# Moving two splits in the first batch of a fused attention and expert kernel

## The chip, the cores and the metric

The kernel runs on one core of one Trainium2 chip. The metric is the device time of one execution in microseconds (us), lower is better. The core has five engines that run side by side, each through its own queue in order: TensorE (PE, matrix products), VectorE (DVE), ScalarE (ACT), GpSimd (POOL) and SyncE (SP, which only issues transfers).

## The reference, cut to what matters

Three blocks follow one another. Four batches of 576 tokens go through an attention with 32 memory slots and 8 heads; its result, 512 numbers per token, goes through a dense MLP with a hidden width of 2048, and that result through 8 experts, two for each token.

```python
def _moe_ref(x, w_in, w_out):          # 2304 tokens, 512 -> 2048 -> 512
    h = x @ w_in
    g = h * (1.0 / (1.0 + np.exp(-h)))
    return (g @ w_out).astype(np.float32)
```

The change lies in this dense MLP, and in its first batch and the second.

## The kernel before, in words

Every float32 product is made from two parts: a number is split into a high part (a copy that is rounded to the format fp32r, by ACT) and a low part (the number less its high part, by DVE or POOL), and PE adds up three products, high by high, high by low and low by high.

The MLP of one batch is 32 steps, two for each of the 16 slices `f` of 128 hidden columns. Step `2f` takes the first 256 tokens of the batch (i = 0), step `2f + 1` the other 320 (i = 1). `mlp_h(b, f, i)` does one step: six matmuls into a PSUM tile `h` (L288), tanh by ACT (L291), the product `(tanh + 1) * h` by DVE (L293), then the split of 256 columns into `gh` (ACT, L297) and `gl` (DVE, or POOL in every fourth step of the first batch, L298). Where i = 1 the last 64 tokens are split as well, into half of a tile `gc` (ACT L306, DVE L307): the last 64 tokens of batches 0 and 1 share one tile of 128, so do those of batches 2 and 3. `mlp_x(b, f, i)` multiplies `g` with slice `f` of w_out (L313) and runs LAG = 4 steps behind `mlp_h`. The `gc` tiles are read by `mlp_rest` after the last step of batch 1 and of batch 3.

w_in and w_out arrive as float64 and are narrowed on the chip during the MLP of the first batch. One slice of w_out goes through `narrow_wout(f)` in step `2f - 1`: three ACT operations on the staged bits (L211, L212, L227), a join by DVE (L217), a multiplication with the sign by POOL (L232), and then the split into `woh[f]` (ACT, L275) and `wol[f]` (POOL for odd `f`, DVE for even, L276). The tile `wo` between them has two buffers. w_in comes in 8 chunks, `narrow_win` (ACT, DVE), and `project` multiplies it with the attention memory (PE L157, then ACT L263 and DVE L264, tile `wpl`).

In the same steps the attention of the next batch is prepared (`phi_top`, `phi_max`, `memory`, `scores`, `softmax_a`, `softmax_b`, `split`). Which function belongs to which step is written out by hand: `at(step, function, ...)` files it under a step, and each step runs `mlp_x`, `mlp_h` and then the functions filed under it. A scheduler afterwards sets the order of each engine's queue from this sequence and from its own estimate of when operands are ready; `tc.issue_after(x)` puts the instructions of a block behind `x` in the queue of x's engine.

Of the kernel before, what the change touches and what calls it, by code (L numbers as in the profile page):

```python
# [6 lines left out]
F32 = mybir.dt.float32  # L7
# [4 lines left out]
AF = mybir.ActivationFunctionType  # L12
OP = mybir.AluOpType
# [3 lines left out]
DM, FF, E, FE = 512, 2048, 8, 1024  # L17
# [3 lines left out]
NF = FF // 128  # L21
# [23 lines left out]
def body(ctx, tc, a):  # L45
    nc = tc.nc
    pe, act, dve, pool, sp = nc.tensor, nc.scalar, nc.vector, nc.gpsimd, nc.sync
# [8 lines left out]
    def psum(tag, bufs):  # L56
        return ps.tile([128, 512], F32, name=tag, tag=tag, bufs=bufs)
# [18 lines left out]
    m1 = moe1.enter_context(tc.tile_pool(name="m1", bufs=1))  # L76
    ap_ = att.enter_context(tc.tile_pool(name="att", bufs=1, side="right"))
# [108 lines left out]
    def turn(b, g, t0, w):  # L186
        AU[b, g] = ap_.tile([128, S], F32, name="att", bufs=2)
        return dve.transpose(AU[b, g][:, :w], AT[b][:, g].rearrange("p a m -> p (a m)")[:, t0:t0 + w])

    def halves(b, g, t0, w):  # L190
        u = AU.pop((b, g))[:, :w]
        if (b, g) not in AH:
            AH[b, g] = [m1.tile([128, S], F32R, name=f"ah{i}", bufs=3) for i in range(2)]
        hi, lo = (x[:, t0:t0 + w] for x in AH[b, g])
        last = act.activation(hi, u, AF.Copy)  # L195
        dve.tensor_sub(lo, u, hi.bitcast(F32))
        return last

    def split(b, g, t0, w):
        turn(b, g, t0, w)  # L200
        halves(b, g, t0, w)


    def stage(src):
        t = m1.tile([128, 512, 2], I32, name="st", tag="st", bufs=4)
        sp.dma_start(t.rearrange("p a w -> p (a w)").rearrange("p (c x) -> p c x", c=src.shape[1]), src)
        return t

    def shrink(t, m):
        low = ap_.tile([128, 512], I32, name="lw", bufs=1)  # L210
        act.activation(low, t[:, :, 0].bitcast(U32), AF.Copy, scale=LOW, bias=LOWB)  # L211
        act.activation(m, t[:, :, 1].bitcast(F32), AF.Copy, scale=2.0 ** -112)  # L212
        return low

    def join(m, low):
        mi = m.bitcast(I32)
        return dve.scalar_tensor_tensor(mi, mi, 3, low, op0=OP.logical_shift_left, op1=OP.bitwise_or)  # L217

    def sign(t, m):
        mi = m.bitcast(I32)  # L220
        dve.scalar_tensor_tensor(mi, t[:, :, 1], -2 ** 31, mi, op0=OP.bitwise_and, op1=OP.bitwise_or)

    def narrow(t, m, own=False):
        low = shrink(t, m)
        if not own:
            g = ap_.tile([128, 512], BF16, name="cg", bufs=1)
            act.activation(g, t[:, :, 1].bitcast(F32), AF.Sign)  # L227
        join(m, low)
        if own:
            sign(t, m)  # L230
        else:
            pool.tensor_mul(m, m, g)  # L232
# [36 lines left out]
    def fetch_wout(i):  # L269
        ST["o", i] = stage(wout[:, i:i + 1, :])  # L270

    def narrow_wout(i):
        w = ap_.tile([128, DM], F32, name="wo", bufs=2)
        narrow(ST.pop(("o", i)), w)
        act.activation(woh[i], w, AF.Copy)  # L275
        (pool if i % 2 else dve).tensor_sub(wol[i], w, woh[i].bitcast(F32))  # L276

    G, X2, GC = {}, {}, {}

    def mlp_h(b, f, i):  # L280
        t0, w = T0[i], TW[i]
        hi, lo = WP[(b * NP + f // 2) // 2]
        c = (f % 4) * 128
        p = psum("h", 2)
        n = 0
        for g in range(2):
            for wt, at in ((hi, 0), (hi, 1), (lo, 0)):
                pe.matmul(p[:, :w], wt[:, g, c:c + 128], AH[b, g][at][:, t0:t0 + w], start=(n == 0), stop=(n == 5))  # L288
                n += 1
        th = m1.tile([128, 320], F32, name="th", bufs=2)  # L290
        act.activation(th[:, :w], p[:, :w], AF.Tanh, scale=0.5)  # L291
        u = th
        dve.scalar_tensor_tensor(u[:, :w], th[:, :w], 1.0, p[:, :w], op0=OP.add, op1=OP.mult)  # L293
        if i == 0:
            G[b, f] = [m1.tile([128, MAIN], F32R, name=f"g{x}", bufs=LAG // 2 + 1) for x in "hl"]
        gh, gl = (x[:, i * 256:(i + 1) * 256] for x in G[b, f])
        act.activation(gh, u[:, :256], AF.Copy)  # L297
        last = (pool if b == 0 and (2 * f + i) % 4 == 0 else dve).tensor_sub(gl, u[:, :256], gh.bitcast(F32))  # L298
        if b:
            LATEST[0] = last  # L300
        if i == 1:
            if (b // 2, f) not in GC:
                GC[b // 2, f] = [m1.tile([128, 128], F32R, name=f"gc{f}_{x}") for x in range(2)]
            ch, cl = GC[b // 2, f]
            r = slice((b % 2) * 64, (b % 2) * 64 + 64)
            act.activation(ch[:, r], u[:, 256:], AF.Copy)  # L306
            dve.tensor_sub(cl[:, r], u[:, 256:], ch[:, r].bitcast(F32))  # L307

    def accumulate(key, terms, f):
        if f == 0:  # L310
# [568 lines left out]
        softmax_b(0, T0[1], TW[1])  # L879
    with tc.issue_after(ready.ins):  # L880
        narrow_wout(0)
    split(0, 0, T0[1], TW[1])
    split(0, 1, T0[1], TW[1])
    with tc.issue_after(ready.ins):
# [4 lines left out]
    def at(s, fn, *args):  # L889
        hooks.setdefault(s, []).append((fn, args))  # L890
# [6 lines left out]
    for f in range(1, NF):  # L897
        at(max(0, 2 * f - 5), fetch_wout, f)
        at(2 * f - 1, narrow_wout, f)
    SB = 2 * NF  # L900
    at(8, routing_setup)
    for b in range(1, B):
        s = (b - 1) * SB
        at(s + (1 if b > 1 else 4), load_phi, b)
# [25 lines left out]
        for i in range(0, NP, 2):  # L930
            for x in range(2):
                at(s + SB - 8 + 4 * i, fetch_win, b * NP + i + x)
            at(s + SB - 4 + 4 * i, project, b * NP + i, 2)
    for b in range(B - 1):
        s = (b + 1) * SB + LAG
        for d in range(4):
# [5 lines left out]
        if b == 1:  # L942
# [3 lines left out]
            at(s + 6, tile_d, j)  # L946
    s = 3 * SB
    at(s, open_a)
    at(s - SB + 10, clear)
    for j in range(EARLY):  # L950
# [8 lines left out]
    def run_h(s):  # L959
        if s < total:  # L960
            mlp_h(s // SB, s % SB // 2, s % 2)
# [19 lines left out]
    while s < total + LAG + 6:  # L981
# [4 lines left out]
        if s in (2 * SB, 4 * SB):  # L986
            b = s // SB - 1
# [83 lines left out]
```

## Time and profile before

| | us |
|---|---|
| median of three runs | 849.98 |
| lowest and highest of them | 848.54, 850.69 |
| the profiled execution, its own time | 845.91 |
| its span, first to last instruction | 844.1 |
| PE busy in the span | 807.1 |

The profile is of one execution. The span is shorter than the execution's own time by what lies around the first and the last instruction. "Busy" is the time in which an engine has an instruction running; instructions of one engine overlap a little at their ends. An "idle before" with an arrow names what the engine waited for.

### The profile page before, as it was taken

How to read it: one execution, taken by the hardware profiler on the slowest of the kernel's cores; microseconds unless marked ns; L12 is line 12 of the kernel's file. 1: busy time of each engine (PE TensorE's matmuls, PEld its weight loads, DVE VectorE, ACT ScalarE, POOL GpSimd, SP SyncE). 2: the span in 40 equal slices, each digit the busy share in tenths (PEclk: the TensorE clock that was granted, in tenths of full speed). 3: DMA queues.
4: the chain of work that ended last, by engine and by line, in shares of the span. 5: the costliest groups of instructions: out<-in, count | busy, mean ns of one | idle time of the engine just before them, and what ended most of it. 6: DMA issues, size and time to landing. Idle time of an engine off the chain costs nothing.

```text
span 844.1 us, 14185 instructions
## 1 busy us (share of the span) xinstructions
PE 807.1 (96%) x5260; PEld 691.4 (82%) x5260; DVE 496.8 (59%) x1178; ACT 360.8 (43%) x856; POOL 209.9 (25%) x237
## 2 busy tenths in 40 slices
PE   4589999999999999999999999999999999999996
PEld 2267678878887888887988989989989899898995
DVE  4898996884268747655724555354553654546521
ACT  3689975444333454553414433324332333233410
POOL 1254530021000400400541504215133142241301
PEclk9599999999999999999999999999999999999999
DMA  9889852543074215232456893765748647586201
GB/s 304 291 295 325 283 217 71 159 131 94 7 229 153 51 51 151 57 82 50 113 138 187 257 257 124 185 237 171 188 169 221 241 139 160 198 220 196 74 4 53
DMA packets 85935, 137.84 MB, mean 163 GB/s; under 512 B 14045, under 2 KB 48349, under 8 KB 85856
## 3 DMA queue, kind: packets, MB, share of 16 engines
q1 hardware_dynamic: 74656, 104.41, 40.9%
q0 software_dynamic: 11200, 32.43, 12.7%
q8 instruction: 43, 0.70, 0.4%
q14 instruction: 36, 0.29, 0.1%
HBM read 106.13 MB, written 31.26 MB: 163 GB/s over the span
## 4 chain that ended last, share of the span: by engine, by line
PE 81%; DVE 9%; ACT 4%; DMA 3%; issue 2%; POOL 1%; SPq 0%; POOLq 0%; ACTq 0%; DVEq 0%
PE x L706 25%; PE x L313 18%; PE x L682 13%; PE h L682 12%; PE h L288 9%; PE aux L157 2%; DMA st<-moe_w_out 1%; DVE th L293 1%; DVE gl L298 1%; DMA kx<-kx 1%; ACT lw L211 1%; POOL wo L232 1%; DMA st<-moe_w_in 1%; DVE mx L113 1%; DVE wo L217 1%
## 5 line engine op out<-in xcount | busy, mean ns | idle before, releaser
L706 PE MATMUL x<-w,gh 128*128 128x512 f32 (+1 forms) x608 | 188.1, 390 | 0.0
L706 PEld LDWEIGHTS x<-w,gh 128*128 128x128 f32 (+1 forms) x608 | 112.4, 186 | 24.3
L682 PE MATMUL h<-xh,w 128*128 128x304 f32 (+4 forms) x512 | 118.7, 304 | 0.0
L706 PE MATMUL x<-w,gl 128*128 128x512 f32 (+1 forms) x304 | 118.5, 390 | 0.0
L682 PE MATMUL x<-xh,w 128*128 128x304 f32 (+4 forms) x512 | 118.1, 302 | 0.0
L288 PE MATMUL h<-ah,wph 128*128 128x320 f32 (+1 forms) x512 | 109.3, 302 | 3.8 <-DVE th L293 1.7
L313 PE MATMUL x<-gh,woh 128*128 128x512 f32 x256 | 105.5, 412 | 0.0
L288 PEld LDWEIGHTS h<-ah,wph 128*128 128x128 f32 x512 | 90.0, 192 | 18.2 <-ACT ah L195 3.6
L721 POOL DMA_INDIRECT out<-y,tab x40 | 41.9, 1049 | 243.1 <-DVE y L716 187.3
L313 PE MATMUL x<-gl,woh 128*128 128x512 f32 x256 | 100.7, 393 | 0.7 <-DVE gl L298 0.7
L313 PE MATMUL x<-gh,wol 128*128 128x512 f32 x256 | 101.2, 395 | 0.0
L293 DVE SCALAR_TENSOR_TENSOR th<-th,h 128x256 f32<-128x256 f32 (+1 forms) x128 | 57.6, 450 | 53.0 <-ACT th L291 52.5
L497 POOL DMA_INDIRECT tab_d<-rows,slot x36 | 40.6, 1128 | 191.3 <-DVE slot L494 177.9
L682 PEld LDWEIGHTS h<-xh,w 128*128 128x128 f32 x512 | 87.3, 188 | 0.6
L682 PEld LDWEIGHTS x<-xh,w 128*128 128x128 f32 x512 | 87.4, 188 | 0.0
L291 ACT ACTIVATE th<-h 128x256 f32<-128x256 f32 (+1 forms) x128 | 52.3, 408 | 73.4 <-PE h L288 71.3
L288 PE MATMUL h<-ah,wpl 128*128 128x256 f32 (+1 forms) x256 | 76.6, 300 | 2.3 <-DVE wpl L264 2.3
L682 PE MATMUL x<-xl,w 128*128 128x304 f32 (+4 forms) x256 | 78.0, 305 | 0.0
L682 PE MATMUL h<-xl,w 128*128 128x304 f32 (+4 forms) x256 | 77.7, 303 | 0.0
L297 ACT ACTIVATE gh<-th 128x256 fp32r<-128x256 f32 x128 | 53.3, 416 | 55.7 <-DVE th L293 55.3
L298 DVE TENSOR_TENSOR gl<-th,gh 128x256 fp32r<-128x256 f32 x120 | 55.1, 459 | 32.0 <-ACT gh L297 28.1
L716 DVE SCALAR_TENSOR_TENSOR y<-x,tab,ex 128x512 f32<-128x512 f32 (+2 forms) x35 | 26.2, 749 | 71.4 <-PE x L706 71.4
(189 smaller groups left out, 1342.0 us busy)
## 6 DMA issues: line engine op xcount, KB each, us to landing
w2s<-moe_w SPq DMA_DIRECT2D x32, 512.0 KB, 8.5
wi<-win_d SPq DMA_DIRECT2D x24, 512.0 KB, 5.1
w1s<-moe_w SPq DMA_DIRECT2D x24, 512.0 KB, 6.2
kv<-kv SPq DMA_DIRECT2D x16, 520.0 KB, 7.3
st<-moe_w_in SPq DMA_DIRECT2D x16, 512.0 KB, 5.2
st<-moe_w_out SPq DMA_DIRECT2D x16, 512.0 KB, 5.9
xs_d<-ex SPq DMA_DIRECT2D x25, 256.0 KB, 3.6
x_d<-xs SPq DMA_DIRECT2D x36, 128.0 KB, 2.4
```

Of the source, the lines that this page charges most:

```text
L157: pe.matmul(p[g][h * M:(h + 1) * M], KVT[b][r, t, h * M:(h + 1) * M], moving(h)[r], start=True, stop=True)
L288: pe.matmul(p[:, :w], wt[:, g, c:c + 128], AH[b, g][at][:, t0:t0 + w], start=(n == 0), stop=(n == 5))
L291: act.activation(th[:, :w], p[:, :w], AF.Tanh, scale=0.5)
L293: dve.scalar_tensor_tensor(u[:, :w], th[:, :w], 1.0, p[:, :w], op0=OP.add, op1=OP.mult)
L297: act.activation(gh, u[:, :256], AF.Copy)
L298: last = (pool if b == 0 and (2 * f + i) % 4 == 0 else dve).tensor_sub(gl, u[:, :256], gh.bitcast(F32))
L313: pe.matmul(X2[key], held, moved, start=(f == 0 and n == 0), stop=(f == NF - 1 and n == 2))
L497: st = pool.indirect_dma_start(out=tab_d, out_offset=bass.IndirectOffsetOnAxis(ap=slot[:, j, k:k + 1], axis=0), in_=rows.bitcast(I32)[:, j ...
L682: pe.matmul(p[:, :w], wt[:, d, c], x[:, d, r], start=(n == 0), stop=(n == 11))
L706: mm = pe.matmul(p, g, w[:, f, :], start=(n == 0), stop=(n == (15 if both else 23)))
L716: done = dve.scalar_tensor_tensor(y, p[:P], w, EX[k, j], op0=OP.mult, op1=OP.add)
L721: st = pool.indirect_dma_start(out=a["out"], out_offset=bass.IndirectOffsetOnAxis(ap=TAB[k][:P, j, 0:1], axis=0), in_=y, in_offset=None, b ...
```

## The change

Two things are moved.

First, in batch 0 the last 64 tokens of each slice `f` are left unsplit in a wide tile `UR`, at a column offset that falls by 64 with each `f`, so that the next slice overwrites only the 256 columns that are done with. The split of slices 0 to 14 (`halve_rest`, one ACT and one DVE instruction each) is filed under steps 38 to 52, the steps 6 to 20 of batch 1, and queued behind the `gh` and `gl` of the step. Slice 15 is split at once, as are all slices of the later batches. The tile `th` with two buffers becomes `TH` for i = 0 and `UR` for i = 1.

Second, `narrow_wout` ends with POOL's multiplication; the split into `woh` and `wol` becomes `halve_wout(f)` and is filed one step later, under step `2f`.

```diff
     def narrow_wout(i):
-        w = ap_.tile([128, DM], F32, name="wo", bufs=2)
+        w = WO[i] = ap_.tile([128, DM], F32, name="wo", bufs=2)
         narrow(ST.pop(("o", i)), w)
+
+    def halve_wout(i):
+        w = WO.pop(i)
         act.activation(woh[i], w, AF.Copy)
         (pool if i % 2 else dve).tensor_sub(wol[i], w, woh[i].bitcast(F32))
 
+    TH = m1.tile([128, 256], F32, name="th")
+    UR = m1.tile([128, 256 + NF * 64], F32, name="ur")
+
+    def rest0(b, f):
+        return 256 if b else 256 + (NF - 1 - f) * 64
...
-        th = m1.tile([128, 320], F32, name="th", bufs=2)
-        act.activation(th[:, :w], p[:, :w], AF.Tanh, scale=0.5)
+        th = (UR[:, rest0(b, f) - 256:] if i else TH)[:, :w]
+        act.activation(th, p[:, :w], AF.Tanh, scale=0.5)
         u = th
...
-        act.activation(gh, u[:, :256], AF.Copy)
+        LAST[0] = act.activation(gh, u[:, :256], AF.Copy)
         last = (pool if b == 0 and (2 * f + i) % 4 == 0 else dve).tensor_sub(gl, u[:, :256], gh.bitcast(F32))
+        LAST[1] = last
...
-            ch, cl = GC[b // 2, f]
-            r = slice((b % 2) * 64, (b % 2) * 64 + 64)
-            act.activation(ch[:, r], u[:, 256:], AF.Copy)
-            dve.tensor_sub(cl[:, r], u[:, 256:], ch[:, r].bitcast(F32))
+            if b or f == NF - 1:
+                halve_rest(b, f)
+
+    def halve_rest(b, f, after=None):
+        u = UR[:, rest0(b, f):rest0(b, f) + 64]
+        ch, cl = GC[b // 2, f]
+        r = slice((b % 2) * 64, (b % 2) * 64 + 64)
+        with tc.issue_after(after[0].ins) if after else ExitStack():
+            act.activation(ch[:, r], u, AF.Copy)
+        with tc.issue_after(after[1].ins) if after else ExitStack():
+            dve.tensor_sub(cl[:, r], u, ch[:, r].bitcast(F32))
...
         narrow_wout(0)
+        halve_wout(0)
...
         at(2 * f - 1, narrow_wout, f)
+        at(2 * f, halve_wout, f)
     SB = 2 * NF
+    for f in range(NF - 1):
+        at(SB + 6 + f, halve_rest, 0, f, LAST)
```

## Rows read from the trace of the kernel before

**Rows 1.** The page: span, and each engine's busy time, share and instructions.

```profile
span 844.1 us, 14185 instructions
...
PE 807.1 (96%) x5260; PEld 691.4 (82%) x5260; DVE 496.8 (59%) x1178; ACT 360.8 (43%) x856; POOL 209.9 (25%) x237
```

**Rows 2.** Windows: length, busy PE, PEld, DVE, ACT, POOL (instructions), clock, DMA share, GB/s.

```profile
37.00:131.00 94.00, 86.25 (x624) 66.57 (x625) 86.08 (x167) 79.29 (x187) 40.83 (x38) 0.98 0.79 271
...
75.00:90.00 15.00, 14.87 (x101) 11.51 (x102) 11.94 (x27) 13.49 (x33) 6.72 (x8) 1.00 0.98 333
...
144.00:180.00 36.00, 35.23 (x313) 28.95 (x312) 28.92 (x103) 14.81 (x41) 2.07 (x2) 1.00 0.51 159
```

**Rows 3.** Waits of PE, 37 to 131: total us, times, longest.

```profile
PE h L288 <- DVE wpl L264: 2.3, 2, 1.2
PE h L288 <- DVE th L293: 1.7, 3, 0.8
...
PE x L313 <- DVE gl L298: 0.7, 1, 0.7
...
PE aux L122 <- DVE mt L120: 0.7, 1, 0.7
```

**Rows 4.** Waits of ACT, 37 to 131, same columns.

```profile
ACT woh L275 <- POOL wo L232: 5.4, 8, 1.2
...
ACT th L291 <- DVE gc L307: 0.4, 1, 0.4
```

**Rows 5.** Windows of L307 alone (DVE), then of L306 alone (ACT).

```profile
37.00:131.00 94.00, 8.31 (x16) 0.98 0.79 271
131.00:213.00 82.00, 3.48 (x16) 1.00 0.40 117
...
37.00:131.00 94.00, 3.97 (x16) 0.98 0.79 271
```

**Rows 6.** Timeline of DVE: start, length, instruction, wait before it.

```profile
43.20 1.19 DVE L307 TENSOR_TENSOR gc<-th,gc 128x64 fp32r<-128x64 f32 x1
...
46.04 1.64 DVE L217 SCALAR_TENSOR_TENSOR wo<-wo,lw 128x512 int32<-128x512 int32 x1
...
49.20 0.21 DVE L307 TENSOR_TENSOR gc<-th,gc 128x64 fp32r<-128x64 f32 x1
49.33 0.41 DVE L293 SCALAR_TENSOR_TENSOR th<-th,h 128x256 f32<-128x256 f32 x1
...
59.35 1.19 DVE L307 TENSOR_TENSOR gc<-th,gc 128x64 fp32r<-128x64 f32 x1
60.46 0.41 DVE L293 SCALAR_TENSOR_TENSOR th<-th,h 128x256 f32<-128x256 f32 x1
60.79 0.28 DVE L120 TENSOR_REDUCE mt<-aux 128x1 f32<-128x128 f32 x1
...
101.44 1.19 DVE L307 TENSOR_TENSOR gc<-th,gc 128x64 fp32r<-128x64 f32 x1
102.55 0.68 DVE L217 SCALAR_TENSOR_TENSOR wo<-wo,lw 128x512 int32<-128x512 int32 x1
...
124.61 1.19 DVE L307 TENSOR_TENSOR gc<-th,gc 128x64 fp32r<-128x64 f32 x1
```

**Rows 7.** Timeline of POOL.

```profile
45.83 1.31 POOL L276 TENSOR_TENSOR wol<-wo,woh 128x512 fp32r<-128x512 f32 x1 [1.51 <-ACT woh L275]
...
57.51 1.63 POOL L276 TENSOR_TENSOR wol<-wo,woh 128x512 fp32r<-128x512 f32 x1 [0.98 <-ACT woh L275]
59.10 1.36 POOL L232 TENSOR_TENSOR wo<-wo,cg 128x512 f32<-128x512 f32 x1
...
101.37 1.18 POOL L232 TENSOR_TENSOR wo<-wo,cg 128x512 f32<-128x512 f32 x1 [0.68 <-DVE wo L217]
```

**Rows 8.** Timeline of PE: first use of `wol` of slices 1 and 3.

```profile
48.21 0.40 PE L313 MATMUL x<-gh,wol 128*128 128x512 f32 x1
...
59.83 0.40 PE L313 MATMUL x<-gh,wol 128*128 128x512 f32 x1
```

## What the change was expected to do

> **What bounds the kernel now.** I read the page first. PE is busy for 807.1 of 844.1 us [rows 1], so over the whole kernel it is the bound, and a change on another engine can pay only where PE stands still. I then cut the span into windows to find those places. The MLP of the first batch, from 37 to 131 us, is the one that this change touches: 94 us with 86.25 busy on PE, so 7.75 us of standing still [rows 2]. In the same window DVE is busy for 86.08 us and ACT for 79.29 us, with the transfers at 0.79 of the DMA engines [rows 2]: no single engine is the bound there, PE and DVE are neck and neck, and ACT is close behind. From 75 to 90 us it is PE itself, 14.87 of 15 us [rows 2].
>
> Next I asked whom PE waits for in this window. Nearly all the waits name DVE: 2.3 us for `wpl`, 1.7 for the tanh product, 0.7 for `gl`, 0.7 for `mt` [rows 3]. With two more rows of the same view (0.7 and 0.3 us) PE's waits for DVE come to 6.4 us, six rows in all. So at the margin the work of DVE sets the end of this batch. Behind it PE goes on almost without a gap: 35.23 of 36 us from 144 to 180 us [rows 2]. What the first batch gains should therefore reach the end of the kernel.
>
> Then the waits of ACT: 5.4 us in eight waits of `woh` for POOL's multiplication [rows 4]. ACT's queue is in order, so the next tanh and the next `gh` stand behind each of these waits, and DVE waits for them in turn.
>
> Last, the timeline of DVE. The subtraction that makes the low part of `gc` writes 64 columns and takes 0.21 us when alone, and the next instruction starts 0.13 us after it [rows 6]. But five of the 16 in this window, the first at 43.20 and the last at 124.61, take 1.19 us [rows 6]. The one at 59.35 ends with POOL's multiplication that began at 59.10 and lasted 1.36 us, and the one at 101.44 with POOL's at 101.37, 1.18 us [rows 6, 7]. A subtraction with both inputs in SBUF waits there until POOL is done. That explains why 16 small subtractions cost 8.31 us here and 3.48 us in the second batch [rows 5]: 5 x 1.19 + 11 x 0.21 = 8.3.
>
> **The change, part by part.**
>
> *The 15 subtractions on DVE.* Those of slices 0 to 14 leave the window; that of slice 15, a short one, stays. Ten short ones at 0.13 us of the queue give 1.3 us. Five long ones hold the queue for 1.11 us each (59.35 to 60.46 [rows 6]), 5.55 us. Not all of it comes free: behind the one at 101.44 comes a join (L217) at 102.55 [rows 6], and a join also waits for POOL, for one of them took 1.64 us at 46.04 beside POOL's subtraction of 45.83 [rows 6, 7]. It would take over about 1.0 us of that wait. The one at 59.35 is followed by the tanh product, 0.41 us, which reads PSUM and shows no such wait [rows 6]; the other three are followed by the same instruction in the timeline, so I count them as free. The sum is 1.3 + 5.55 - 1.0 = 5.9 us of DVE. If all long waits are handed on, it is 15 x 0.13 = 2.0 us; if none, 6.9 us.
>
> *Why this reaches PE.* At 59.35 the long subtraction stands ahead of `mt` at 60.79, for which PE waits 0.7 us [rows 3, 6]. It also delays the next tanh product, from which PE's h matmuls get their PSUM tile. These gaps are bounded by the 6.4 us in which PE waits for DVE. From 75 to 90 us time on DVE buys nothing, since PE has no gap there: 79/94 of 5.9 us is 5.0 us.
>
> *The 15 copies on ACT.* They are 3.97 / 16 = 0.25 us each [rows 5], at most 3.7 us, and one of the DVE subtractions held up a tanh for 0.4 us [rows 4]. PE's own waits for ACT are small, so I count these at nothing by themselves: they pay by feeding DVE, whose 5.0 us is already counted. If that cover is wrong, and ACT is what holds DVE back, up to 6.4 us can be had in all.
>
> *`woh` and `wol` one step later.* Nothing is removed; the eight waits of ACT, 5.4 us, can be filled with the next step's tanh and `gh`. That too feeds DVE and is counted at nothing above the 5.0 us. Behind it is a danger: what is late next is `wol`. For slice 1 POOL ends it at 45.83 + 1.31 = 47.14 and PE reads it at 48.21, 1.07 us later; for slice 3 it is 57.51 + 1.63 = 59.14 and 59.83, 0.69 us [rows 7, 8]. The mean step is 94 / 32 = 2.9 us. The later slices are split further ahead of their use. If the scheduler keeps `woh` as soon as POOL's product is there, nothing is lost; a whole step later costs 1.8 + 2.2 = 4.0 us. No row shows which. The instruction only yields to work that is ready, so I am near the low end and take 0.5 us. The two buffers of `wo` are held a step longer, but the product that needs one back comes two slices later.
>
> *The 15 splits in batch 1.* They add 15 x 0.22 = 3.3 us to DVE (3.48 / 16 each [rows 5]) and 3.7 us to ACT between about 144 and 180 us. There DVE is busy 28.92 and ACT 14.81 of 36 us, and POOL, which made the waits, only 2.07 [rows 2]. PE's gap there is 0.77 us. What hides them is the four steps by which `mlp_x` runs behind. Uncovered they cost 15 x 0.13 = 2.0 us of DVE's queue; covered nothing. I take 0.5 us.
>
> *The tiles.* `TH` and `UR` are reused after two steps, as the two buffers of `th` were. No transfer is added or moved past another. I count nothing.
>
> The sum is 5.0 - 0.5 - 0.5 = 4.0 us. The profiled execution, 845.91 us with 1.8 us around its span, would become 841.9. It is 4.07 us faster than the median of the runs, 849.98, to which the forecast refers: **846.0 us**.
>
> **The rule that speaks against it.** The row shows 1.19 us beside POOL against 0.21 us alone [rows 6]. The Trainium skill says in "SBUF — State Buffer", section "Who interferes with whom", that a DVE instruction with two SBUF inputs contends with a GpSimd instruction that reads SBUF, and that the one issued second is blocked for the whole of the other. The trace agrees: 1.19 us ends with POOL's instruction. By that rule POOL's own instructions, which the change leaves as many and as long, block whichever such DVE instruction comes next, so the sum would be 2.0 us and not 5.9.
>
> **The rivals.**
>
> *The waits are handed on.* The place of each long subtraction is taken by the next `gl`, join or `wol` that meets POOL. For it: POOL works 40.83 of 94 us [rows 2], and the joins wait as well (1.64 us). Against: four of five times what follows reads PSUM. DVE gains 2.0 us, less 0.5 in batch 1: 848.5 us. It is what the rule above would make of it. Chance 0.20.
>
> *The staged transfers set the pace.* Then faster narrowing only waits for the next slice. For it: the DMA engines are at 0.98 from 75 to 90 us. Against: they are at 0.79 over the batch [rows 2], and no wait of PE leads straight to them. I give it a gain of 1 us, 849.0 us. Chance 0.10.
>
> *Slower: `wol` comes late.* With a lag of L for slices 1 and 3, PE loses 2L - 1.76 us. At one step this only eats the gain (849.98 - 4.5 + 4.0 = 849.5). It turns to slower by over 0.3% when 2L - 1.76 exceeds 4.5 + 2.55, so at L = 4.4 us, and at the 5.9 us of a whole slice it is 10.0 us, 855.5 us. For it: only about 1 us of room, and the split is filed behind the projection in its step. Against: POOL stood idle for 1.51 and 0.98 us before these two subtractions, waiting for ACT [rows 7], so for a lag of 4.4 us ACT would have to put other ready work ahead of `woh` for a step and a half. Chance 0.12.
>
> **How the numbers follow.** The forecast has 0.58. About 0.3%, 2.55 us, is what a measurement can tell here. Faster is the forecast alone, 0.58; the same is the two rivals in the middle, 0.30; slower is the late `wol`, 0.12. The likeliest case by itself runs from 843.0 (6.4 us of gaps and half of 0.77 given back) to 847.4 us. For the range I take 1 us below the former for the scatter of the runs, and 851.0 above, which takes in both middle rivals and a lag of one step with the highest run.
>
> **What would show it.** The line of L307 should have one instruction in the first batch and 31 in the second, none of the moved ones near 1 us. ACT's waits of `woh` for POOL should fall from 5.4 us to below 2. The MLP of batch 0 should end about 4 us earlier, with PE's waits for DVE nearer 3 than 6 us, and the same 713 us or so behind it. I am wrong if other DVE instructions beside POOL grow by as much, if PE waits for `wol` at slices 1 and 3, or if the scheduler's new order opens a gap that none of these rows shows.

## The result, and the profile after

The changed kernel is slower: 855.16 us in the median of six runs, against 850.36 us for the kernel before in six runs beside it. The ratio is 1.0056, with an interval of [1.0043, 1.0069]. Timed again beside the kernel before, on three chips, it came to 1.0038, 1.0035 and 1.0033, all of them above 1.002 at the lower end of the interval. Four single executions of 1037 to 1608 us in these sets and the experiments were disturbed and are left out everywhere. The forecast was 846.0 us, that is 0.995: the sign was wrong.

The first of the two moves came out as forecast, the second only in part. Windows of the changed kernel (columns as in [rows 2]), then of its L329 alone, which is L307 of before, the `gc` subtraction:

```profile
37.00:131.00 94.00, 83.85 (x597) 63.92 (x598) 80.36 (x145) 75.03 (x166) 39.82 (x38) 0.96 0.79 271
...
120.00:131.00 11.00, 8.87 (x64) 6.69 (x65) 8.14 (x14) 4.31 (x10) 0.92 (x2) 0.84 0.44 156
144.00:180.00 36.00, 35.22 (x319) 28.24 (x319) 28.52 (x109) 16.55 (x52) 0.00 (x0) 1.00 0.49 156
...
37.00:136.00 99.00, 0.22 (x1) 0.97 0.75 258
136.00:218.00 82.00, 6.18 (x31) 1.00 0.39 117
```

One `gc` subtraction is left in the first batch, where there were 16 [rows 5], and the 31 in the second take 0.20 us each. `woh` is another matter. Counted by the tanhs that stand ahead of it in ACT's queue, one for each step, only that of slice 8 comes a step later than before; ten keep their step, and five come earlier, that of slice 15 by four steps. Within its step it stands further back, up to 3.1 us behind POOL's product where it was 0.8. The scheduler did not keep the step under which the split was filed.

DVE works 80.36 us in the 94 us, 5.72 less than before [rows 2], but it also gets less done there: 145 instructions against 167, of which only 15 were moved away. The 148 other DVE instructions that lie in this window before are busy for 79.9 us before and for 82.5 us in the changed kernel (82.1 and 82.4 in two later profiles). For the same work DVE is thus freed of about 3 us. Most of the difference is in the 31 joins (L217), before and after:

```profile
20.00:140.00 120.00, 22.87 (x31) 0.91 0.74 251
...
20.00:140.00 120.00, 25.00 (x31) 0.97 0.73 251
```

The second batch has no new gap: PE is busy 35.22 of 36 us from 144 to 180 us, as before. But PE gets through less, not more, in the first batch, 597 matmuls in the 94 us against 624 [rows 2]. Waits of PE, then of ACT, from 37 to 136 us (total, times, longest), to be read against [rows 3] and [rows 4]:

```profile
PE h L302 <- DVE wpl L264: 3.0, 2, 2.7
PE h L302 <- DVE ur L307: 2.1, 3, 0.9
PE aux L157 <- DVE wpl L264: 1.8, 2, 1.6
PE aux L157 <- DVE phi L125: 1.2, 1, 1.2
...
ACT woh L280 <- POOL wo L232: 1.4, 4, 0.5
```

ACT's waits of `woh` for POOL did fall, from 5.4 to 1.4 us. PE's waits for DVE rose: to the four rows here come 0.8 us for `gl` and 0.6 for `mt`, 9.5 us in all against 6.4. The longest is now 2.7 us, and no wait of PE in the kernel before lasted over 1.21 us there. Timeline of that place, PE, DVE and POOL (L312 is L298 of before, `gl`; L302 is L288, h; L281 is L276, `wol`):

```profile
119.07 0.40 PE L302 MATMUL h<-ah,wph 128*128 128x256 f32 x2
122.13 0.38 PE L302 MATMUL h<-ah,wpl 128*128 128x256 f32 x1 [2.67 <-DVE wpl L264]
122.45 1.93 PE L157 MATMUL aux<-wi,kvt 64*32 64x256 f32 x32
...
124.90 0.63 PE L335 MATMUL x<-gh,wol 128*128 128x512 f32 x1
...
126.55 0.45 PE L302 MATMUL h<-ah,wph 128*128 128x320 f32 x2
...
118.38 0.41 DVE L264 TENSOR_TENSOR wpl<-aux,wph 128x256 fp32r<-128x256 f32 x1
118.72 0.36 DVE L183 RECIPROCAL ssm<-ssm 128x36 f32<-128x36 f32 x1
119.17 1.31 DVE L312 TENSOR_TENSOR gl<-th,gh 128x256 fp32r<-128x256 f32 x1
120.40 1.35 DVE L184 TENSOR_TENSOR sct<-sct,ssm 128x1152 f32<-128x1152 f32 x1
121.67 0.41 DVE L264 TENSOR_TENSOR wpl<-aux,wph 128x256 fp32r<-128x256 f32 x1
...
118.90 1.29 POOL L281 TENSOR_TENSOR wol<-wo,woh 128x512 fp32r<-128x512 f32 x1 [0.74 <-ACT woh L280]
```

The same place in the kernel before, and POOL's `wol` of slice 15 there:

```profile
116.75 0.40 PE L288 MATMUL h<-ah,wph 128*128 128x256 f32 x2
118.36 0.39 PE L288 MATMUL h<-ah,wpl 128*128 128x256 f32 x1 [1.21 <-DVE wpl L264]
118.67 1.09 PE L157 MATMUL aux<-wi,kvt 64*32 64x256 f32 x32
...
120.03 0.40 PE L313 MATMUL x<-gh,wol 128*128 128x512 f32 x1
...
121.19 0.46 PE L288 MATMUL h<-ah,wph 128*128 128x320 f32 x2
...
116.01 0.36 DVE L264 TENSOR_TENSOR wpl<-aux,wph 128x256 fp32r<-128x256 f32 x1
116.29 1.34 DVE L184 TENSOR_TENSOR sct<-sct,ssm 128x1152 f32<-128x1152 f32 x1
117.55 0.41 DVE L298 TENSOR_TENSOR gl<-th,gh 128x256 fp32r<-128x256 f32 x1
117.89 0.41 DVE L264 TENSOR_TENSOR wpl<-aux,wph 128x256 fp32r<-128x256 f32 x1
...
126.45 1.30 POOL L276 TENSOR_TENSOR wol<-wo,woh 128x512 fp32r<-128x512 f32 x1 [0.74 <-ACT woh L275]
```

In both, PE waits at one h matmul for the second of two `wpl`, and in both a softmax product (L184) and a `gl` stand between the two in DVE's queue. After the change two things differ. The reciprocal L183 also stands between them, and POOL's `wol` of slice 15 now runs beside that `gl`, which takes 1.31 us instead of 0.41. This `wol` did not come later but earlier, at 118.90 us instead of 126.45: the new order brings the narrowing of the last slice forward. And behind the gap of 2.67 us PE runs slower. The same work, from the L157 group to the next h matmul, takes 126.55 - 122.45 = 4.10 us instead of 121.19 - 118.67 = 2.52, and a 512-column matmul takes 0.63 us instead of 0.40. The granted clock is 0.84 from 120 to 131 us; before it was 1.00 there.

To see where the loss arises, I follow three matmuls in time, counted from PE's first h matmul of step 1 (37.59 us in the profile of before), in the profile of before and in three profiles of the changed kernel:

| matmul (its start before) | before | after | second | third |
|---|---|---|---|---|
| L122, second group (69.51) | 31.92 | 34.52 | 31.48 | 32.51 |
| h, last ahead of the gap (116.75) | 79.16 | 81.51 | 78.69 | 80.00 |
| L122 of a later batch (250.84) | 213.25 | 218.34 | 215.48 | 215.87 |

From row 2 to row 3 the changed kernel loses 2.7, 2.7 and 1.8 us (each column's difference to before in row 3 less that in row 2). Of each, 0.3 us arise in the second batch, the rest at the place near 120 us. The first profile lost 2.6 us earlier, between 60 and 72 us, where DVE's queue held a narrowing of w_in that waited for its transfer ahead of the tanh product; the second profile lost nothing there and the third 0.6. The span of the first, 855.1 us, is 11 us above that of before: 5.1 us are these, and the other 6.0 arise at stalls of PE far behind (354 to 456 us) that follow no wait: the lag is 5.06 us ahead of them, 9.40 behind the first and 11.02 behind the last. They seem to be no part of the change's price. The third profile has such stalls too, 4.0 us, and so has that of an altered kernel from the same chip, where the kernel before also takes 850 us in the median; the profiles from chips where it takes 845 us have none, nor has the first one of before, whose execution took 845.91 us.

### The profile page after: what moved, and what is told of

It reads as the page before. It is cut to its first block, busy times and chain, and to the rows that moved or that the text cites. A ratio compares the mean times of both kernels' runs of the same rounds, so it can differ in the third digit from the quotient of the medians.

```text
span 855.1 us, 14182 instructions
## 1 busy us (share of the span) xinstructions
PE 811.7 (95%) x5260; PEld 694.3 (81%) x5260; DVE 495.3 (58%) x1178; ACT 360.6 (42%) x856; POOL 206.4 (24%) x237
## 4 chain that ended last, share of the span: by engine, by line
PE 82%; DVE 9%; ACT 3%; DMA 2%; issue 2%; POOL 1%; SPq 0%; POOLq 0%; ACTq 0%; DVEq 0%
PE x L728 25%; PE x L335 18%; PE x L704 12%; PE h L704 12%; PE h L302 9%; PE aux L157 2%; DMA st<-moe_w_in 1%; DMA st<-moe_w_out 1%; DVE mx L113 1%; PE aux L136 1%; DVE gl L312 1%; DVE wo L217 1%; DMA phi<-phi 1%; PE aux L681 1%; DVE g L473 1%
## 5 line engine op out<-in xcount | busy, mean ns | idle before, releaser
L302 PE MATMUL h<-ah,wph 128*128 128x320 f32 (+1 forms) x512 | 109.9, 303 | 6.4 <-issue 2.6
L302 PEld LDWEIGHTS h<-ah,wph 128*128 128x128 f32 x512 | 90.6, 193 | 21.1 <-issue 3.7
L519 POOL DMA_INDIRECT tab_d<-rows,slot x36 | 38.3, 1063 | 204.9 <-DVE slot L516 191.5
L302 PE MATMUL h<-ah,wpl 128*128 128x256 f32 (+1 forms) x256 | 76.8, 301 | 3.0 <-DVE wpl L264 3.0
L728 PEld LDWEIGHTS x<-w,gl 128*128 128x128 f32 (+1 forms) x304 | 56.4, 186 | 12.6
L335 PEld LDWEIGHTS x<-gh,woh 128*128 128x128 f32 x256 | 48.8, 191 | 18.4 <-issue 10.2
L335 PEld LDWEIGHTS x<-gl,woh 128*128 128x128 f32 x256 | 48.7, 190 | 13.8 <-issue 1.5
L714 DVE SCALAR_TENSOR_TENSOR gl<-h,gh 128x304 fp32r<-128x304 f32 (+4 forms) x64 | 30.4, 474 | 49.0 <-ACT gh L713 39.8
```

What stands on the lines that cost most here:

```text
L335: pe.matmul(X2[key], held, moved, start=(f == 0 and n == 0), stop=(f == NF - 1 and n == 2))
L519: st = pool.indirect_dma_start(out=tab_d, out_offset=bass.IndirectOffsetOnAxis(ap=slot[:, j, k:k + 1], axis=0), in_=rows.bitcast(I32)[:, j ...
L714: LATEST[0] = dve.scalar_tensor_tensor(l, p, 0.0, h.bitcast(F32), op0=OP.max, op1=OP.subtract)
L728: mm = pe.matmul(p, g, w[:, f, :], start=(n == 0), stop=(n == (15 if both else 23)))
```

## The experiments

Two theories were set against each other first. **A:** the two edits do what they were meant to, but the scheduler, whose estimates they alter, built other queues, and these open gaps for PE. **B:** the moved work itself costs the time (late `wol`, or the splits in batch 1).

**Each half alone.** First only the deferred `gc`:

```diff
-        at(2 * f, halve_wout, f)
+        at(2 * f - 1, halve_wout, f)
```

> The deferral alone: the last 64 tokens are left unsplit, woh and wol follow the narrowing in the same step as before. Theory A (the queue order): what costs is the order that the scheduler makes anew. Here DVE's queue has wpl of the eighth pair (slices 14 and 15) behind the softmax product and behind a gl, as in the changed kernel, so PE should stand for 2 us or more near 120 us, but the join of w_in is not pulled ahead near 60 us. Expected 849 to 853 us. Theory B (the later halves of w_out cost): nothing is lost here and the freed DVE time is gained, 845 to 848 us.

Measured 1.0036 [1.0022, 1.0049]. Then only the later split of w_out:

```diff
-            if b or f == NF - 1:
-                halve_rest(b, f)
+            halve_rest(b, f)
...
-    for f in range(NF - 1):
-        at(SB + 6 + f, halve_rest, 0, f, LAST)
```

> The shift alone: woh and wol one step later, every slice split at once as before. Theory A: the queues have the narrowing of w_in ahead of the tanh product near 60 us, as in the changed kernel, so ACT should wait there for a transfer of w_in by about 2 us and PE lose 1 to 2 us; wpl stands where it stood before, so no long gap near 120 us. Expected 851 to 854 us. Theory B: the whole loss is here, 855 us or more, with PE waiting for wol or woh.

Measured 1.0032 [1.0020, 1.0043]. Either half alone costs about as much as both together, which does not fit costs that belong to the moved work and add up. PE's longest gaps lay elsewhere in each: 1.65 us before `mt` at 61 us in the first, which did not show the long gap at 120 us that I had expected of it; 1.63 us at 81 us and 2.01 us at 107 us in the second. Most of the loss of the first arises at 103 to 106 us, where PE waits 1.20 and 0.82 us for `wpl` and the granted clock is 0.66 from 105 to 110 us.

**Order and work apart.** A table of (line, occurrence) is added to a kernel, and each engine's queue in the first batch is held to it (shortened):

```diff
+    for e, order in ORDER.items():
+        row = [found[e, k] for k in order.split()]
+        for x, y in zip(row, row[1:]):
+            tc.add_manual_dep(y, x.name, NoSync)
```

The work of the changed kernel in the queues of the kernel before (ACT, DVE, POOL and PE):

> The changed kernel's work (15 splits deferred) with the queues of ACT, DVE, POOL and PE held, through the first batch, in the order of the kernel before; the deferred splits are simply missing from them. Theory A: the gain that was forecast appears, since only the order took it away: 846 to 848 us, with PE's gaps at mt and at the tanh product smaller. Theory C (the freed DVE time is worth nothing, because waits for POOL or for transfers take its place): within 1 us of the kernel before, 849.5 to 851.

And the work of the kernel before in the queues of the changed one:

> The kernel before, all its splits in place, with the queues of ACT, DVE, POOL and PE held in the order of the changed kernel through the first batch; each gc split stands behind the gh and the gl of its step. Theory A: the order alone costs, and without the relief it costs more than the change did: 855 to 860 us. Theory C or B: the order by itself is harmless, 850 to 852 us.

Measured: 0.9985 [0.9976, 0.9994] and 1.0086 [1.0072, 1.0100]. The new order with the work of before costs 7.1 us. The first kernel gains 1.2 us, which lies between what theories A and C expected. Its table also holds `woh` and `wol` at their old places, so it is the deferral alone, and in the old order nothing is lost by it: that half of theory B falls. The other half, a late `wol`, falls by the traces: PE has no wait for `woh` or `wol` in the changed kernel. Theory A's core holds, that the order by itself costs time.

No kernel was held in its own order, so what holding does by itself is not measured. It seems to be little: the changed kernel's order, held with one `woh` moved, took 1.0031 beside 1.0035 for the changed kernel itself on one chip (below).

But 1.2 us is far less than the 4.0 us forecast. The window and the waits of DVE in that kernel, 37 to 131 us:

```profile
37.00:131.00 94.00, 87.97 (x627) 69.28 (x628) 80.41 (x151) 77.30 (x172) 39.94 (x37) 0.95 0.79 271
...
DVE gl L312 <- ACT gh L311: 3.2, 6, 1.5
DVE wol L281 <- ACT woh L280: 2.6, 4, 1.0
DVE wi L217 <- ACT lw L211: 2.2, 3, 1.7
DVE ur L307 <- ACT ur L305: 1.8, 2, 1.0
```

and the waits that answer to them in the kernel before:

```profile
DVE th L293 <- ACT th L291: 2.0, 3, 1.0
DVE gl L298 <- ACT gh L297: 1.7, 4, 0.6
DVE wol L276 <- ACT woh L275: 1.6, 2, 1.0
...
DVE wi L217 <- ACT lw L211: 0.2, 1, 0.2
```

DVE is freed of 86.08 - 80.41 = 5.67 us, as forecast; the 148 other instructions take 79.8 us here, as before. Its waits for ACT, eight rows against six, rise from 6.7 to 12.2 us: nearly the whole of it is spent there. This profile is of the slowest of the kernel's eleven executions, 845.62 us where the median is 843.28, so the gain itself is not in it. In the profile of the same kernel with `woh` and `wol` free (843.46 us, below) the waits for ACT come to 10.6 us, and in a second profile of before to 7.3. So they take up more than half of the freed time, and how much more is not settled.

**Where in the order.** The work of before, in the new order up to about 85 us and the old one behind, and the reverse:

> Work of the kernel before (woh, wol and gc in their own steps); the queues of ACT, DVE, POOL and PE stand in the changed kernel's order up to about step 16 of the first batch (about 85 us), in the order before behind it. Whole new order on this work cost 7.1 us (ratio 1.0086). Theory A (the order costs at two places that add up, near 60 to 70 us and near 120 us): half of it, 3 to 4 us, ratio 1.004, with PE's gaps at 63 and 69 us there and none over 1.5 us behind 100 us. Rival B (one place near 120 us, where PE falls to half clock, carries it all): ratio 1.000 to 1.001.

> The same work; the order before up to about step 16, the changed kernel's order behind it. Theory A: the other half, 3 to 4 us, ratio 1.004, with a gap of 2 us near 122 us and the gaps at 63 and 69 us gone. Rival B: the whole 7 us, ratio 1.008.

Measured 1.0033 [1.0021, 1.0045] and 1.0057 [1.0044, 1.0071]. They add up to 1.0090, near the whole order's 1.0086. So the order costs in both halves, with the larger part behind 85 us, and rival B falls. The places are more than theory A's two. The first kernel has gaps of 1.43 us at 63 us, 0.96 at 69 and 1.19 at 81 us; the second waits for `wpl` 1.75 us at 104 us and 2.19 us at 121 us. The changed kernel itself waits 0.56 us at the first of these places and not at the third, so a part of the 7.1 us is paid only by the old work in the new order.

**What eats the freed time.** The whole change in the old order, but with `woh` and `wol` left free:

> The whole change with the queues in the order before (0.9985 when measured alone), but w_out's split (woh on ACT, wol on DVE and POOL) is left free, so that it comes where the change puts it, about a step later. Theory C (the 5.7 us that DVE is freed of are eaten by ACT's 5.0 us of waits for POOL's multiplication, which DVE then waits for): ACT's waits for POOL fall under 2 us, and 1.5 to 3 us more are gained, ratio 0.995 to 0.9965. Rival D (PE's waits in the first batch hang on other things, so that the later split brings nothing): ratio 0.998 to 0.9995.

Measured 0.9986 [0.9977, 0.9995]: nothing more is gained. This does not refute theory C. Left free, `woh` hardly moved: twelve of the 16 keep their place in ACT's queue, four come one or two instructions later, and ACT's waits for POOL only fell from 5.0 to 4.3 us. No run tested a split that comes a whole step later for all slices. The kernel below with one `wpl` moved has only 1.3 us of these waits and gains nothing on the kernel before either. That speaks against them as the limit, but its order differs in much else.

**The place near 120 us.** The changed kernel in its own order, with one instruction of DVE's queue moved:

```diff
-wpl #15, L183, gl #20, L184, wpl #16
+wpl #15, wpl #16, L183, gl #20, L184
```

> The changed kernel as it is, queues in its own order, but the 16th subtraction of wpl stands directly behind the 15th on DVE, ahead of a gl and of the softmax product that stood between. Theory A (PE's 2.7 us gap at 122 us is this place in DVE's queue, and its half clock behind it follows from the gap): gap under 0.5 us, 2 to 3 us gained, ratio 1.002 to 1.0035 against 1.0056 of the changed kernel. Rival E (the gap only moves on to the softmax product or the gl, which are late by the same): ratio stays at 1.005 to 1.006.

Measured 1.0005 [0.9996, 1.0014], more than theory A asked for. The changed kernel had not been timed beside it, and was timed again, on another chip:

> The changed kernel unaltered, beside the runs it is to be compared with. If the 1.0005 of its own order with one wpl moved is the move's doing (theory A), this run stays at 1.005 to 1.0065 and shows the 2.7 us gap of PE near 122 us again. If the chip did it (rival), the ratio comes out near 1.001 and the gap is shorter than 1 us.

It stayed slower (1.0038 [1.0024, 1.0051]) and showed the gap, 2.65 us. To learn whether POOL's `wol` beside the `gl` makes the gap long, `woh` of the last slice was moved on ACT behind a tanh that waits for PE, so that its `wol` comes after that place, as in the kernel before; the changed kernel ran beside it a third time:

```diff
-wph, wph, woh #16, gh, tanh, tanh (waits for PE)
+wph, wph, gh, tanh, tanh (waits for PE), woh #16
```

> The changed kernel in its own order, except that on ACT the last slice's woh stands behind the tanh for which ACT waits 3.1 us near 119 us, so that POOL's wol of that slice no longer runs beside DVE's gl near 116 us. Theory G (the collision of that wol with the gl lengthens PE's gap from 1.2 to 2.65 us and the half clock follows from the length): gl 0.4 us instead of 1.29, gap 1.6 to 1.9 us, 1 to 2.5 us gained on the changed kernel, ratio 1.001 to 1.003 where the changed kernel beside it has 1.004. Rival H (the two instructions ahead of the wpl set the gap, whoever runs beside them): gap above 2.3 us, ratio as the changed kernel's within 0.001.

> The changed kernel unaltered, a third time. If the 2.6 us lost between 62 and 72 us in the first profile belong to single executions: no gap over 0.9 us there and the clock at its upper level from 42 to 115 us, ratio 1.003 to 1.0045. If they belong to the kernel on some chips: the gaps of about 1 us and the lower clock again, ratio 1.005 to 1.006.

Measured 1.0031 [1.0016, 1.0047] and 1.0035 [1.0023, 1.0047], which does not tell the two apart: the runs of the former scattered from 850 to 856 us. In its profiled execution, one of the two quickest, the gap was 0.72 us and the clock behind it stayed; in that of the changed kernel beside it the gap was 1.73 us. The loss between 60 and 72 us came back in part (a gap of 1.16 us for `phi`, 0.6 us lost), without the lower clock. So four kernels were timed side by side on one chip, the last with a second place mended as well: the two `wpl` near 103 us, for which PE waits 1.55 us, made adjacent, with their `wph` ahead of a narrowing on ACT.

> The changed kernel, as the measure of the three beside it: ratio 1.0035 to 1.0055.

> Changed kernel in its own order with the 16th wpl directly behind the 15th, again. If the gap near 120 us is worth what the first run of it showed: 0.3 points below the changed kernel beside it. If that came of comparing different chips: within 0.1 points of it.

> Changed kernel with the last slice's woh behind the tanh on ACT, again. Theory G (the collision of wol with gl makes the gap long): 0.2 to 0.3 points below the changed kernel beside it. Rival (the order of the two instructions ahead of the wpl, or the clock's fall at 103 us instead, costs as much): within 0.1 points of it.

> As the one with the 16th wpl moved, and the 13th and 14th wph and wpl made adjacent and ahead of a narrowing on ACT and of a gl on DVE. If the 1.57 us gap near 103 us and the clock behind it carry the rest of the loss: gap under 1.0 us, ratio 0.9985 to 1.000, level with the order before (0.9985). If the rest sits elsewhere: ratio as the one with a single place mended.

| kernel | median us | ratio | interval |
|---|---|---|---|
| before | 845.02 | 1 | |
| changed | 848.14 | 1.0033 | [1.0021, 1.0046] |
| changed, `woh` #16 behind the tanh | 845.80 | 1.0012 | [1.0003, 1.0021] |
| changed, `wpl` #16 ahead | 845.65 | 1.0004 | [0.9995, 1.0013] |
| changed, both pairs of `wpl` adjacent | 845.28 | 1.0002 | [0.9993, 1.0011] |

Moving one instruction takes back 2.49 of the 3.12 us. Timeline of the kernel with `wpl` #16 ahead, DVE, then POOL, then PE:

```profile
115.35 0.74 DVE L264 TENSOR_TENSOR wpl<-aux,wph 128x256 fp32r<-128x256 f32 x2
116.02 0.36 DVE L183 RECIPROCAL ssm<-ssm 128x36 f32<-128x36 f32 x1
116.30 1.16 DVE L312 TENSOR_TENSOR gl<-th,gh 128x256 fp32r<-128x256 f32 x1
117.38 1.35 DVE L184 TENSOR_TENSOR sct<-sct,ssm 128x1152 f32<-128x1152 f32 x1
...
115.87 1.30 POOL L281 TENSOR_TENSOR wol<-wo,woh 128x512 fp32r<-128x512 f32 x1 [0.74 <-ACT woh L280]
...
116.49 1.09 PE L157 MATMUL aux<-wi,kvt 64*32 64x256 f32 x32
```

The `gl` still meets POOL and takes 1.16 us, and L184 still takes 1.35 us; PE no longer waits for either. With `woh` moved instead, DVE and PE show:

```profile
116.64 0.36 DVE L312 TENSOR_TENSOR gl<-th,gh 128x256 fp32r<-128x256 f32 x1
116.92 1.34 DVE L184 TENSOR_TENSOR sct<-sct,ssm 128x1152 f32<-128x1152 f32 x1
118.18 0.41 DVE L264 TENSOR_TENSOR wpl<-aux,wph 128x256 fp32r<-128x256 f32 x1
...
118.65 0.39 PE L302 MATMUL h<-ah,wpl 128*128 128x256 f32 x1 [1.53 <-DVE wpl L264]
118.97 1.09 PE L157 MATMUL aux<-wi,kvt 64*32 64x256 f32 x32
```

Without POOL beside it the `gl` takes 0.36 us and the gap is 1.53 instead of 2.65 us: the collision with the `wol` that was brought forward accounts for about 1.1 us of the gap (theory G), and on this chip the edit was worth 0.2 points. On the other chip the gap fell by as much, from 1.73 to 0.72 us, but the time did not show it, so the size of the gain rests on one set of runs. Mending the second place as well brought nothing that can be told: the gap near 103 us fell from 1.55 to 1.06 us, one of 0.72 us for the tanh product came at 110 us, and the ratio fell by 0.0002, which is within the interval.

**The old order, mended at the same place.** The change in the old order with `wpl` #16 directly behind #15, and the same with `woh` and `wol` free:

> The whole change under the order before, with the 16th wpl directly behind the 15th on DVE. If PE's wait of 1.1 us for it near 118 us is on the path: gap gone, 1 us more gained than under the order before alone (0.9985), ratio 0.997 to 0.998. If the gl and the softmax product that it overtakes are as much on the path: 0.9985, with PE waiting for ah or for the tanh product 1 us later instead.

> Order before, w_out's split left free (0.9986 when measured), and the 16th wpl directly behind the 15th. Sum of the parts if they are independent: 1.2 us and 1 us, ratio 0.997 to 0.998. If the transfers into the staging tiles set the pace between 75 and 100 us, nothing behind them adds: 0.9985 as without it.

Measured 0.9983 [0.9974, 0.9993] and 0.9982 [0.9973, 0.9991], medians 843.70 and 843.80 us beside 844.95 for before. They beat both kernels, but the move adds nothing that can be told from 0.9985: PE's wait for `wpl` near 118 us went, and one of 1.1 us for `ah`, which stands behind the two instructions that were overtaken, came in its place in both.

A second profile of the kernel before, for the scatter:

> A second profile of the kernel before, for the scatter of one profile. The start of the first matmul of the second batch's transposes (250.84 us in the first profile) should come back within 1 us; the time at which TensorE's clock rises in the first batch (41 us in the first profile, 46 us in four of the altered ones) tells whether that belongs to the kernel (41 again) or to the execution (either).

The L122 matmul came back at 249.55 us, 212.93 counted from the first h matmul of step 1 against 213.25. The clock was 0.50 from 40 to 45 us, where it had been 0.86, so the time of its rise belongs to the execution.

## Why the prediction was wrong

- **The price of the subtractions was right in the old order.** 5.9 us of DVE were forecast, and 5.67 left the window there. In the changed kernel's own order only about 3 us were freed for the same work, since the joins and other instructions took 2.2 to 2.6 us longer. So the rival that hands the waits on, 2.0 us, is false in the old order and about half right in the new one. The rule behind it, the Trainium skill's in "SBUF — State Buffer", section "Who interferes with whom", is real: the trace agrees at the `gl` of 1.31 us beside POOL's `wol`, against 0.36 us once the `wol` is gone.
- **"79/94 of 5.9 us is 5.0 us" was the over-sized term.** With the order kept, the deferral gains 1.2 us (0.5 to 2.0 by the interval), not 4.0. The step took PE's 6.4 us of waits for DVE as time that a faster DVE would remove. In the old order they fell only to 4.6 us, where a second profile of before has 5.1, and DVE's own waits for ACT grew, by 3 to 5.5 us. ACT is busy 77 of 94 us there; I had read it as "close behind", and then counted it as no limit. That ACT is the limit is argued from these waits and not shown. What in turn sets its pace, POOL's products, the transfers of w_in (one wait of 1.9 us at 85.6 us in the old order) or its own 77 us, the runs did not separate. So the rival of the staged transfers, with its gain of 1 us, stays open.
- **The missing term was the queues, and it turned the sign.** The prediction named a new order of the scheduler in its last sentence and gave it no price and no chance, and priced every other step as if each instruction kept its place. The new order costs 7.1 us with the old work, and more than the deferral gains with the new. Its worst place is the one near 120 us, where two more things delay `wpl` #16 and the clock falls behind the gap: putting that one instruction ahead takes the ratio from 1.0033 to 1.0004. Why the first set of runs gave 1.0056 and the later ones 1.0033 to 1.0038 is not settled; its profile lost 2.6 us more between 60 and 72 us.
- **The late `wol`, the rival on the slower side, did not occur.** POOL's `wol` of slice 3 ended at 56.59 + 1.62 = 58.21 us and PE read it at 58.91, no wait. What did harm was a `wol` that came earlier, that of slice 15, and not because PE needed it but because it ran beside a `gl`. ACT's waits for POOL fell below 2 us as said, and that fed DVE nothing that reached PE.
- **The splits in batch 1 cost 0.3 us; 0.5 were forecast.** From 140 to 185 us PE's lag behind before grows from 4.78 to 5.06 us in the changed kernel. It grows by 0.25 to 0.30 us in every profiled kernel that defers the splits, and by at most 0.03 in those that do not.
- **One sum of the range is off.** 849.98 less 6.4 and half of 0.77 is 843.2 us and not 843.0, which changes nothing here.

## What to carry to other kernels

Where a scheduler rebuilds the queues from estimates, an edit's price has two parts, the work and the order, and they can be measured apart: run the new work in the old order and the old work in the new. Read in the trace, too, where a moved instruction came to stand: the `woh` that was filed a step later mostly did not come a step later. Freed time on an engine that shares the bound with a second one (86 and 79 of 94 us here) should be counted only after the second one's waits are followed too; here one fifth of it reached the end. And look first for the one instruction for which the bound engine waits longest, and for what stands ahead of it in its queue: moving that one was worth 2.5 us, twice the gain of the deferral in the old order.

## What the runs showed of the hardware that was not expected

**A gap of PE is paid twice, or not.** Behind the gap of 1.21 us near 118 us before and of 0.72 us in one altered kernel the granted clock stayed at its upper level (2.4 GHz, written 1.00). Behind those of 1.53, 1.73, 2.65 and 2.67 us at the same matmul it was 0.66 to 0.76 in the window from 120 to 125 us, in which part of the matmuls ran at the lower level, and a 512-column matmul took 0.63 us instead of 0.40. The length alone does not decide: behind a gap of 1.55 to 1.6 us near 103 us the clock fell in the third profile of the changed kernel (0.75 from 105 to 110 us) and stayed in the first two. With the later split alone it stayed at 1.00 behind a gap of 2.01 us at 107 us. In the two kernels that hold the old work to the new order up to 85 us there is the same gap of 1.19 us at 81 us, and from 80 to 85 us the clock was 1.00 in one and 0.67 in the other.

**The clock rose at different times in executions of one order, at no cost.** The old work in the new order throughout and the old work in the new order up to 85 us run the same queues at the start. Windows from 42 to 46 us and the same h matmul in the first:

```profile
42.00:46.00 4.00, 4.00 (x13) 3.44 (x13) 3.97 (x9) 3.59 (x10) 1.96 (x3) 0.50 0.94 303
...
53.82 0.41 PE L288 MATMUL h<-ah,wph 128*128 128x320 f32 x1 [0.42 <-DVE th L293]
```

and in the second:

```profile
42.00:46.00 4.00, 3.59 (x20) 2.67 (x20) 3.97 (x9) 3.57 (x10) 1.91 (x3) 1.00 0.99 331
...
53.87 0.42 PE L288 MATMUL h<-ah,wph 128*128 128x320 f32 x1 [0.42 <-DVE th L293]
```

In one the clock is at 1.2 GHz in that window, in the other at 2.4 GHz, and 16.25 us behind the first h matmul of step 1 (37.57 and 37.62 us) both are at the same matmul: DVE is busy 3.97 of the 4 us in both and sets the pace, and a slower PE only fills what was idle. PE's busy share says nothing there (4.00 against 3.59 us); a window has to be read with its clock.
